# Spreading w1, w2 conversions and a, b units over steps 10 to 20, and reordering the loads and banks of M

## The chip, the cores and the metric

The kernel runs on one core of a Trainium2 chip. The metric is the device time of one execution in microseconds (us), as the median of the executions that were timed. TensorE (PE, with its weight loads PEld), VectorE (DVE), ScalarE (ACT) and GpSimd (POOL) each take their instructions in the order in which the program lists them; SyncE (SP) issues all DMAs of this kernel, also in order.

## The reference

Attention with a learned decay bias, then two feed-forward stages. All matrices arrive as 64-bit or 32-bit floats; the kernel splits each 32-bit operand into a rounded high word and a remaining low word (suffixes h and l) and adds three products (hh, hl, lh) for each product of matrices.

```python
bias   = -(cum[:, :, :, None] - cum[:, :, None, :])            # cum = cumsum(relu(s))
attn   = softmax(causal(q @ k.T * scale + min(bias, 0)))       # 4 batches x 8 heads, 576 x 576
x      = (attn @ v) heads side by side                         # 2304 x 512
h      = ((x @ w1) * (x @ w2)) @ w3                            # 1024 wide
y      = h @ w_out                                             # 512 wide
h2     = y @ w_in;  solu = h2 * softmax(h2);  ln = layer norm of solu, times g_ln
out    = ln @ w_out2                                           # 2304 x 512
```

The kernel multiplies w3 and w_out together first: M = w3 @ w_out, so that y = ((x @ w1) * (x @ w2)) @ M.

## The kernel before

**Order of the work.** The kernel is written in program order and a scheduler lays out each engine's list of instructions at build time: it prefers what stands earlier in the program, but takes a later instruction where, by its own reckoning of time, the earlier one isn't ready. The list is fixed then; on the chip an engine waits at the head of its list even where the next instruction could run. `tc.issue_after(ins)` (line 383 for one) forces an instruction behind another on the same engine.

**Steps.** Lines 534 to 598 run 36 steps. A step does the scores and softmax of one head (`qk_part`, `softmax_tile`, lines 180 to 214), the normalising and transposing of the head two before it (`normalise`, `tr_part`) and, for each pair of heads, probabilities times v (`av_parts`, line 265). Steps 0 to 9 take batch 0; from step 10 on, head h is done in step h + 2. Beside the heads run the a, b units of the batch before: `ab_unit(n, f, half)` at line 293 is 12 matmuls of x @ w1 for a block f of 128 columns and half the tokens, evicted by ACT to `a_sb` (line 315), and 12 of x @ w2, multiplied by `a_sb` on DVE into `g_sb` (line 323). `NF` (line 538) says how many units a step receives, and its 16 units of batch 0 (blocks f = 0 to 7, two halves) stand in steps 10 to 20.

**Conversions.** Blocks of w1 and w2 are loaded raw by `stage` (line 375, two buffers `stage` in this part) and converted from 64 bits by `to_f32` (ACT line 340, DVE lines 346, 347, 351) and split (`hi` on ACT line 93, `lo` on DVE line 98), which frees the buffer for the next load. `jobs` holds them in order: w1 block 0, w2 block 0, w1 block 1, and so on, 16 in all; unit block f needs jobs 2f+1 and 2f+2. `PUMP` (line 540) says how many conversions a step gets: steps 3, 5 and 6 one each, steps 10 to 15 two each, step 16 one. In steps, a conversion is also held behind the first softmax tile of that step's head (`behind`, line 195, line 399). The other half of the splitting, that of q and k, goes to POOL (`split_qk`, line 160).

**PSUM.** Steps use `bigtile` (tag A, two banks a tile: scores' first tile and `av`) and `smalltile` (tag B, one bank: everything else). Up to step 10 they are `psA` (2 tiles) and `psB` (4); from step 11 `psE` (1 tile, two banks) and `psF` (6).

**M.** After the steps the a, b units of the last batch run (lines 640 to 648) with the conversions of w_out and the first w3 blocks. Then psE and psF are closed and replaced by `psC` (tiles X, Y, Z, W for the second stage) and `psD` (4 small tiles), lines 651 to 655. Lines 896 to 906 build M: `load_g(0)` loads the first chunk of g, five `wf_load` load words of w_in that earlier steps had prepared, `load_g(1)` the second chunk; then for each of 8 blocks `m_unit(f)` does 24 matmuls of 512 columns and evicts MH and ML, `pump(AM[f])` converts two more w3 blocks (blocks 0 to 4) from four buffers, and `wf_words(f)` (line 885) splits one word for f below 6. After M, `x2_half` (line 698) multiplies g by M, and `h_pair` (line 846) the result by the words of w_in (`IT`, seven matrices in two halves, 14 words) on tiles X, Y, Z, W. The remaining eight of 22 words are those of w_out2 (OH, OL).

**End.** `out_unit(t)` (line 831) does 24 matmuls of 512 columns for 128 tokens, evicts them on ACT to `o` and stores them.

Of the kernel before, what the change touches and what calls it, by code (L numbers as in the profile page):

```python
# [26 lines left out]
def tile_attention_moe(  # L27
# [29 lines left out]
    for i in (2, 3, 1, 4, 0):  # L57
# [3 lines left out]

    dram = ctx.enter_context(tc.tile_pool(name="dram", bufs=1, space=DRAM))
    ps_ctx = ExitStack()
    PSP = [
        ps_ctx.enter_context(tc.tile_pool(name="psA", bufs=2, space=PSUM)),
        ps_ctx.enter_context(tc.tile_pool(name="psB", bufs=4, space=PSUM)),
    ]
    const = ctx.enter_context(tc.tile_pool(name="const", bufs=1, side="left"))
# [21 lines left out]

    def hi(dst, src, eng=None):
        if eng is None:
            nc.scalar.activation(out=dst, in_=src, func=AF.Copy)  # L93
        else:
            eng.tensor_copy(out=dst, in_=src)

    def lo(dst, src, hi_, eng=nc.vector):
        eng.tensor_tensor(out=dst, in0=src, in1=hi_.bitcast(F32), op=ALU.subtract)  # L98


    attn_ctx = ExitStack()
# [269 lines left out]
    loaded = []  # L371

    stg = [at, 2]

    def stage(src):
        raw = stg[0].tile([128, CW, 2], U32, tag="stage", bufs=stg[1], name="stage")
        dst = flat(raw)
        if len(src.shape) == 3:
            dst = dst.rearrange("p (c f) -> p c f", c=src.shape[1])
        if after[0] is None:  # L380
            nc.sync.dma_start(out=dst, in_=src)
        else:
# [155 lines left out]
    NF = {10: 3, 11: 0, 12: 3, 13: 0, 14: 3, 15: 2, 16: 2, 17: 0, 18: 1, 19: 1, 20: 1, 21: 2, 22: 2, 23: 2, 24: 2, 25: 2, 26: 2, 27: 2, 28: 2, 29: 2, 30: 2, 31: 2, 32: 2, 33: 2, 34: 3, 35: 3}  # L538
    PD, FS = 10, 0.5
    PUMP = {3: 1, 5: 1, 6: 1, 10: 2, 11: 2, 12: 2, 13: 2, 14: 2, 15: 2, 16: 1}  # L540
    PUMP.update((i, 1 if i < 30 else 2) for i in range(22, 34))
    fill = []
    late = []
    for st, (h, ph) in enumerate(steps):
# [3 lines left out]
        if st == 11:  # L548
            ps_ctx.close()
            PSP[:] = [  # L550
                ps_ctx.enter_context(tc.tile_pool(name="psE", bufs=1, space=PSUM)),
                ps_ctx.enter_context(tc.tile_pool(name="psF", bufs=6, space=PSUM)),
            ]

# [64 lines left out]
        w_job(w3L[f, :, 1024 * i:1024 * i + 1024], dst)  # L619

    def m_unit(f):
        ps = smalltile("m")
        for k in range(KF):
            H3, L3 = m_st[f, k // 4]
            for w_, o_ in ((H3, WOH), (H3, WOL), (L3, WOH)):
                nc.tensor.matmul(
                    ps, w_[:, k % 4], o_[:, k],
                    start=(k == 0 and w_ is H3 and o_ is WOH), stop=(k == KF - 1 and w_ is L3),
                )
        hi(MH[:, f], ps)  # L630
        lo(ML[:, f], ps, MH[:, f])
# [8 lines left out]
    for i in range(8):  # L640
# [8 lines left out]
    behind.clear()  # L649
    right0.close()  # L650
    ps_ctx.close()
    PSP[:] = [
        ctx.enter_context(tc.tile_pool(name="psC", bufs=1, space=PSUM)),
        ctx.enter_context(tc.tile_pool(name="psD", bufs=4, space=PSUM)),
    ]
    HD = DF // 2

    r2 = ctx.enter_context(tc.tile_pool(name="r2", bufs=1, side="right"))
# [171 lines left out]

    def out_unit(t):
        LH, LL = lt_t.pop(t)
        ps = smalltile("o")
        for k in range(KF):
            for l_, w_ in ((LH, OH), (LH, OL), (LL, OH)):
                nc.tensor.matmul(  # L836
                    ps, l_[:, k], w_[:, k],
                    start=(k == 0 and l_ is LH and w_ is OH), stop=(k == KF - 1 and l_ is LL),
                )
        o = p2.tile([128, DM], F32, tag="o", bufs=1, name="o")  # L840
        nc.scalar.activation(out=o, in_=ps, func=AF.Copy)
        nc.sync.dma_start(out=out[t * 128:t * 128 + 128], in_=o)

    NCH = NT // 2

    def h_pair(c):
# [5 lines left out]
        X, Y, Z, W = (PSP[0].tile([128, HD], F32, tag=n, name=f"h{n}") for n in "XYZW")  # L852
        h_mm(X, "A11", "B11", True)
        copy(h0[:, 0:HD], X)
        h_mm(Z, "S1", "T1", True)
# [24 lines left out]
    def wf_load(i):  # L880
        if i < len(WL):
            wf[i] = wpool.tile([128, CW], F32, tag="wf", bufs=5, name="wf")
            nc.sync.dma_start(out=wf[i], in_=wf_scr[WL[i]])
# [9 lines left out]
        lo(l_, t, h_, V)  # L893
        wf_load(i + 5)

    load_g(0)
    for i in range(5):
        wf_load(i)
    load_g(1)
    for f in range(nm[0], KF):  # L900
        m_unit(f)
        pump(AM[f])
        if f < 6:
            wf_words(f)
        if f == 5:
            split_g(0)
    mctx.close()
    p2 = ctx.enter_context(tc.tile_pool(name="p2", bufs=1, side="left"))
    OH = p2.tile([128, KF, DM], F32R, name="OH")
    OL = p2.tile([128, KF, DM], F32R, name="OL")  # L910
    x2_half(0, 0)
    x2_first(0)
    x2_half(0, 1)
    x2_second(0)
    split_g(1)
    for i in range(6, 14):
# [91 lines left out]
```

## Time and profile before

| | us |
|---|---|
| median of 3 executions (731.38 to 734.41) | 731.58 |
| the profiled execution, its own time | 732.8 |
| its span, first to last instruction | 731.1 |
| PE busy in the span | 714.2 (98%) |
| PEld busy | 631.5 (86%) |
| DVE busy | 507.7 (69%) |
| ACT busy | 470.4 (64%) |
| POOL busy | 95.2 (13%) |

The profile is of one execution. Times in rows are us from the span's start unless they are called ns. Matmuls overlap, so that neighbouring ones start before the one ahead has ended. A bracket at the end of a row of the timeline tells how long the engine had been idle and who released it.

### The profile page before, as it was taken

Reading aid. Unit: us, or ns where it says so; the run is one execution under the profiler, and the core shown is the slowest. Engines: PE = TensorE matmul, PEld = TensorE weight load, DVE = VectorE, ACT = ScalarE, POOL = GpSimd, SP = SyncE. Lnnn points to the kernel's source line nnn. Section 1 sums busy time; section 2 is a strip of 40 time slices with the busy share of each in tenths; the row PEclk is TensorE's granted clock in tenths of the full one; section 3 lists DMA queues with packets and bytes.
Section 4 is the critical chain, followed back from the end, with each engine's and each line's share of the span. In section 5 each row is a group of like instructions: output and inputs, shape, how many; then the busy total and the mean of one; then the engine's idle time right before and its main releaser. Section 6 shows DMA issues by size and latency. Waiting matters only on the chain.

```text
span 731.1 us, 12896 instructions
## 1 busy us (share of the span) xinstructions
PE 714.2 (98%) x4618; PEld 631.5 (86%) x4618; DVE 507.7 (69%) x1251; ACT 470.4 (64%) x977; POOL 95.2 (13%) x88
## 2 busy tenths in 40 slices
PE   9989998999999999999998999999999999999997
PEld 6669888889899999999997889988888988888886
DVE  7996989898777887822777966675747366563651
ACT  7996878798676777822544735576737465563742
POOL 3051322234121221000000000001000000000000
PEclk9999999999999999999999999999999999999999
DMA  5644555555476655514566933153324252302311
GB/s 124 190 135 132 156 164 146 164 148 127 140 205 184 207 164 175 179 62 161 185 204 201 378 114 101 59 116 87 79 66 102 45 133 68 87 19 68 66 36 43
DMA packets 79827, 95.50 MB, mean 131 GB/s; under 512 B 41418, under 2 KB 52682, under 8 KB 79764
## 3 DMA queue, kind: packets, MB, share of 16 engines
q1 hardware_dynamic: 79764, 94.69, 44.5%
q8 instruction: 36, 0.59, 0.3%
q14 instruction: 27, 0.22, 0.1%
HBM read 59.04 MB, written 20.14 MB: 108 GB/s over the span
## 4 chain that ended last, share of the span: by engine, by line
PE 81%; DVE 9%; DMA 5%; ACT 2%; issue 2%; SPq 0%; DVEq 0%; ACTq 0%
PE x L710 14%; PE o L836 14%; PE a L303 12%; PE b L303 11%; PE av L275 6%; PE hX L742 5%; PE tr L247 5%; DMA stage<-in_w_dram 4%; PE hZ L742 3%; PE sc L178 2%; PE sc L177 2%; PE hW L742 2%; PE hY L742 2%; DVE stage L351 2%; PE sc L169 1%
## 5 line engine op out<-in xcount | busy, mean ns | idle before, releaser
L190 ACT ACTIVATE P<-P,STAT 64x64 f32<-64x64 f32 (+4 forms) x160 | 88.5, 556 | 22.9 <-DVE STAT L186 22.3
L98 POOL TENSOR_TENSOR QK<-qk,QK 64x1152 fp32r<-64x1152 f32 x24 | 66.2, 2759 | 172.9 <-ACT QK L93 172.8
L710 PE MATMUL x<-gl,MH 128*128 128x256 f32 x288 | 80.4, 279 | 0.0
L710 PE MATMUL x<-gh,ML 128*128 128x256 f32 x288 | 80.2, 279 | 0.0
L710 PE MATMUL x<-gh,MH 128*128 128x256 f32 x288 | 79.9, 279 | 0.0
L303 PE MATMUL b<-xT0h,W 128*128 128x288 f32 x256 | 58.4, 301 | 3.5 <-DVE W L98 2.1
L303 PE MATMUL a<-xT0h,W 128*128 128x288 f32 x256 | 59.2, 306 | 0.0
L247 PE MATMUL tr<-ident,P 128*128 128x128 f32 x416 | 54.4, 275 | 3.5 <-DVE STAT L186 2.7
L303 PE MATMUL a<-xT1h,W 128*128 128x288 f32 x256 | 57.6, 300 | 0.0
L836 PE MATMUL o<-OH,lh 128*128 128x512 f32 x144 | 57.0, 396 | 0.2 <-DVE ll L98 0.2
L836 PE MATMUL o<-OH,ll 128*128 128x512 f32 x144 | 57.0, 396 | 0.0
L836 PE MATMUL o<-OL,lh 128*128 128x512 f32 x144 | 57.0, 396 | 0.0
L303 PE MATMUL b<-xT1h,W 128*128 128x288 f32 x256 | 56.4, 295 | 0.0
L710 PEld LDWEIGHTS x<-gl,MH 128*128 128x128 f32 x288 | 54.1, 188 | 1.5 <-DVE gl L98 0.2
L710 PEld LDWEIGHTS x<-gh,MH 128*128 128x128 f32 x288 | 53.9, 188 | 1.1
L710 PEld LDWEIGHTS x<-gh,ML 128*128 128x128 f32 x288 | 54.0, 188 | 0.9
L806 DVE COPY lt<-turned 128x2048 uint16<-128x2048 uint16 x16 | 22.0, 1373 | 45.4 <-DMA turned<-half 45.4
L247 PEld LDWEIGHTS tr<-ident,P 128*128 128x128 f32 x416 | 46.8, 141 | 5.4 <-issue 1.6
L323 DVE TENSOR_TENSOR g_sb<-b,a_sb 128x288 f32<-128x288 f32 x64 | 28.7, 450 | 31.6 <-PE b L303 21.5
L340 ACT ACTIVATE stage<-stage 128x512 f32<-128x512 f32 x56 | 37.1, 679 | 20.5 <-DMA stage<-in_w_dram 18.7
L226 ACT ACTIVATE P<-P,STAT 128x576 f32<-128x576 f32 x64 | 42.7, 717 | 10.5 <-DVE STAT L219 10.4
L315 ACT ACTIVATE a_sb<-a 128x288 f32<-128x288 f32 x64 | 25.7, 403 | 36.3 <-PE a L303 36.0
(191 smaller groups left out, 1984.1 us busy)
## 6 DMA issues: line engine op xcount, KB each, us to landing
stage<-in_w_dram SPq DMA_DIRECT2D x32, 512.0 KB
g_scr<-g_sb SPq DMA_DIRECT2D x32, 288.0 KB
stage<-in_wo_dram SPq DMA_DIRECT2D x16, 512.0 KB
qk<-in_qk_dram SPq DMA_DIRECT2D x24, 288.0 KB
QK<-QK SPq DMA_DIRECT2D x24, 288.0 KB
gl<-g_scr SPq DMA_DIRECT2D x24, 256.0 KB
wf<-wf_scr SPq DMA_DIRECT2D x22, 256.0 KB
out_dram<-o SPq DMA_DIRECT2D x18, 256.0 KB
```

What stands on the lines that cost most here:

```text
L98: eng.tensor_tensor(out=dst, in0=src, in1=hi_.bitcast(F32), op=ALU.subtract)
L190: ex = nc.scalar.activation(out=dst, in_=dst, func=AF.Exp, bias=st[0:rows, ti:ti + 1], scale=-1.0, accum_out=st[0:rows, 5 + ti:6 + ti],)
L226: nc.scalar.activation(out=dst, in_=src, func=AF.Copy, scale=r)
L247: last_tr[0] = nc.tensor.transpose(ps[:, 128 * n:128 * n + 128], pt[:, o:o + 128], ident)
L275: nc.tensor.matmul(st["ps"][64 * e:64 * e + 64, 448 + c0:448 + c1], vr[:, j, e], PT[(2 * p + e) % 4][:, o + c0:o + c1], **kw,)
L303: nc.tensor.matmul(ps, w_[:, c, fs], x_[:, c, sl], start=(c == 0 and w_ is WH and x_ is XH), stop=(c == KC - 1 and w_ is WL),)
L315: ab_last[0] = nc.scalar.activation(out=a_sb, in_=ps, func=AF.Copy).ins
L323: ab_last[1] = nc.vector.tensor_tensor(out=g[:, sl], in0=ps, in1=st["a"], op=ALU.mult).ins
L340: nc.scalar.activation(out=high.bitcast(F32), in_=high.bitcast(F32), func=AF.Copy, scale=2.0 ** -112)
L710: last = nc.tensor.matmul(ps[:, a], w_[:, k, m * 128:m * 128 + 128], g_[:, k % 2], start=(k == 0 and w_ is MH and g_ is GH), stop=(k == KF ...
L742: last_h[0] = nc.tensor.matmul(ps, x_[:, k], w_[:, k], start=first and k == 0 and x_ is XH and w_ is WH, stop=k == 1 and x_ is XL, skip_gr ...
L836: nc.tensor.matmul(ps, l_[:, k], w_[:, k], start=(k == 0 and l_ is LH and w_ is OH), stop=(k == KF - 1 and l_ is LL),)
```

## The change

The table of units goes from 3, 0, 3, 0, 3, 2, 2, 0, 1, 1, 1 to 2, 1, 2, 1, 2, 1, 2, 1, 2, 1, 1 for steps 10 to 20, that of conversions from 2, 2, 2, 2, 2, 2, 1 in steps 10 to 16 to 2, 1, 2, 1, 2, 1, 2, 1, 1 in steps 10 to 18. The double bank psE goes to the other side of PSUM and stays open over M; M's first block is computed in it, and it becomes tiles X and Y afterwards, while Z, W and psD replace psF. In M the loads of g and of words come behind the raw block that was staged last before them; only words 0 and 1 are split in M, words 2 to 13 behind the last w3 conversion, and the last four words of w_out2 behind the splits of the second stage's first chunk. The last `out_unit` works in two halves of 256 columns, each evicted and stored by itself.

```diff
@@ pools
-        ps_ctx.enter_context(tc.tile_pool(name="psA", bufs=2, space=PSUM)),
+        ps_ctx.enter_context(tc.tile_pool(name="psA", bufs=2, space=PSUM, side="right")),
@@ helpers: hi and lo note their instruction in last_hi[0], last_lo[0]; stage notes its DMA in last_stage[0]
+    def held(*ins):
+        order = ExitStack()
+        for i in ins:
+            order.enter_context(tc.issue_after(i))
+        return order
@@ steps
-    NF = {10: 3, 11: 0, 12: 3, 13: 0, 14: 3, 15: 2, 16: 2, 17: 0, 18: 1, 19: 1, 20: 1, 21: 2, ...}
+    NF = {10: 2, 11: 1, 12: 2, 13: 1, 14: 2, 15: 1, 16: 2, 17: 1, 18: 2, 19: 1, 20: 1, 21: 2, ...}
-    PUMP = {3: 1, 5: 1, 6: 1, 10: 2, 11: 2, 12: 2, 13: 2, 14: 2, 15: 2, 16: 1}
+    PUMP = {3: 1, 5: 1, 6: 1, 10: 2, 11: 1, 12: 2, 13: 1, 14: 2, 15: 1, 16: 2, 17: 1, 18: 1}
@@ step 11
-                ps_ctx.enter_context(tc.tile_pool(name="psE", bufs=1, space=PSUM)),
+                big_ctx.enter_context(tc.tile_pool(name="psE", bufs=1, space=PSUM, side="right")),
@@ m_unit
-        ps = smalltile("m")
+        ps = smalltile("m") if f else bigtile("m")[:, 0]
@@ second stage's banks
-    PSP[:] = [
-        ctx.enter_context(tc.tile_pool(name="psC", bufs=1, space=PSUM)),
-        ctx.enter_context(tc.tile_pool(name="psD", bufs=4, space=PSUM)),
-    ]
+    psp = {}
+    psp["Z"] = psp["W"] = ctx.enter_context(tc.tile_pool(name="psC", bufs=1, space=PSUM))
+    PSP[1] = ctx.enter_context(tc.tile_pool(name="psD", bufs=4, space=PSUM))
@@ M
-    load_g(0)
-    for i in range(5):
-        wf_load(i)
-    load_g(1)
     for f in range(nm[0], KF):
         m_unit(f)
-        pump(AM[f])
-        if f < 6:
-            wf_words(f)
+        if AM[f]:
+            pump(AM[f])
+            w3_last = last_hi[0], last_lo[0]
+        with held(last_stage[0]):
+            if f == 0:
+                load_g(0)
+            elif f == 1:
+                for i in range(5):
+                    wf_load(i)
+            elif f == 4:
+                load_g(1)
+        if 2 <= f < 4:
+            wf_words(f - 2)
         if f == 5:
             split_g(0)
     ...
+    big_ctx.close()
+    psp["X"] = psp["Y"] = ctx.enter_context(tc.tile_pool(name="psG", bufs=1, space=PSUM, side="right"))
     x2_half(0, 0)
     x2_first(0)
     x2_half(0, 1)
     x2_second(0)
+    words_last = last_hi[0], last_lo[0]
     split_g(1)
-    for i in range(6, 14):
-        wf_words(i)
+    with held(*w3_last):
+        for i in range(2, 14):
+            wf_words(i)
     load_g(2)
     ...
-            for i in range(14, 22):
+            for i in range(14, 18):
                 wf_words(i)
+            with held(*words_last):
+                for i in range(18, 22):
+                    wf_words(i)
@@ out_unit
+        for c0, c1 in ((0, DM),) if t < NT - 1 else ((0, DM // 2), (DM // 2, DM)):
+            ps = smalltile("o")[:, 0:c1 - c0]
             ... the matmuls on w_[:, k, c0:c1], the second part behind the first
+            nc.scalar.activation(out=o[:, c0:c1], in_=ps, func=AF.Copy)
+            nc.sync.dma_start(out=out[t * 128:t * 128 + 128, c0:c1], in_=o[:, c0:c1])
```

## Rows read from the trace of the kernel before

**Rows 1.** The page: busy time of each engine, its share of the span, instructions.

```profile
PE 714.2 (98%) x4618; PEld 631.5 (86%) x4618; DVE 507.7 (69%) x1251; ACT 470.4 (64%) x977; POOL 95.2 (13%) x88
```

**Rows 2.** Windows by stage: length, PE, PEld, DVE, ACT, POOL busy, clock, DMA, GB/s.

```profile
57.00:155.00 98.00, 92.66 (x665) 84.84 (x665) 84.34 (x237) 77.72 (x185) 26.29 (x9) 0.97 0.54 158
155.00:389.00 234.00, 234.00 (x1782) 217.97 (x1781) 166.46 (x438) 148.04 (x355) 34.60 (x13) 1.00 0.53 164
389.00:440.00 51.00, 48.15 (x228) 40.01 (x227) 39.47 (x70) 27.51 (x48) 0.00 (x0) 1.00 0.65 227
440.00:700.00 260.00, 260.00 (x1540) 229.43 (x1539) 158.35 (x321) 155.52 (x236) 17.12 (x25) 1.00 0.32 79
```

**Rows 3.** Timeline of PE, the three longest idle spans in 57 to 155.

```profile
92.67 0.52 PE L247 MATMUL tr<-ident,P 128*128 128x128 f32 x3 [1.40 <-DVE STAT L186]
...
120.53 0.40 PE L303 MATMUL b<-xT0h,W 128*128 128x288 f32 x1 [0.76 <-ACT W L93]
...
123.70 0.54 PE L303 MATMUL b<-xT0h,W 128*128 128x288 f32 x2 [2.09 <-DVE W L98]
```

**Rows 4.** Windows around the two stretches of lower clock (columns as in rows 2).

```profile
92.00:99.00 7.00, 6.21 (x34) 6.00 (x35) 6.92 (x25) 5.82 (x18) 3.93 (x1) 0.76 0.52 159
123.00:130.00 7.00, 6.30 (x36) 6.30 (x37) 5.15 (x22) 6.26 (x14) 1.24 (x1) 0.76 0.61 193
```

**Rows 5.** Waits of DVE in 57 to 155: us in total, times, longest.

```profile
DVE stage L346 <- DMA stage<-in_w_dram: 7.0, 5, 1.9
```

**Rows 6.** Timeline of DVE: the raw block ahead of a softmax, and head 12's tile.

```profile
91.42 0.43 DVE L346 TENSOR_SCALAR stage<-stage 128x512 uint32<-128x512 uint32 x1 [0.59 <-DMA stage<-in_w_dram]
91.76 0.62 DVE L186 CUSTOM_DVE_ANT_0 P<-sc,wmask 128x448 f32<-128x448 f32 x1
...
110.25 0.75 DVE L186 CUSTOM_DVE_ANT_0 P<-sc,lmask 128x576 f32<-128x576 f32 x1
```

**Rows 7.** Timeline of DVE and POOL, 118 to 124: head 13's tile and conversion 12.

```profile
118.06 0.75 DVE L186 CUSTOM_DVE_ANT_0 P<-sc,lmask 128x576 f32<-128x576 f32 x1
...
120.74 2.31 DVE L351 SCALAR_TENSOR_TENSOR stage<-stage 128x512 uint32<-128x512 uint32 x1
122.97 0.68 DVE L98 TENSOR_TENSOR W<-stage,W 128x512 fp32r<-128x512 f32 x1
...
119.86 2.64 POOL L98 TENSOR_TENSOR QK<-qk,QK 64x1152 fp32r<-64x1152 f32 x1 [5.71 <-ACT QK L93]
```

**Rows 8.** Conversion steps by shape, 57 to 155 (DVE), and one a unit's matmuls.

```profile
L347 DVE SCALAR_TENSOR_TENSOR stage<-stage 128x512 uint32<-128x512 uint32 x13 | 8.8, 682 | 0.0
...
99.42 1.60 PE a L303 x12
```

**Rows 9.** Timeline of PE and DVE around M's first matmul, and PE's wait at M's end.

```profile
391.99 0.50 PE L626 MATMUL m<-WOH,w3h 128*128 128x512 f32 x1 [2.24 <-DVE g_sb L323]
...
391.49 0.45 DVE L323 TENSOR_TENSOR g_sb<-b,a_sb 128x288 f32<-128x288 f32 x1
...
428.71 0.50 PE L626 MATMUL m<-WOH,w3h 128*128 128x512 f32 x1 [0.61 <-ACT w3h L93]
```

**Rows 10.** Timeline of DVE, 431 to 440, and PE's first use of T1's words.

```profile
434.75 0.69 DVE L98 TENSOR_TENSOR ML<-m,MH 128x512 fp32r<-128x512 f32 x1 [2.95 <-ACT MH L93]
439.86 0.69 DVE L98 TENSOR_TENSOR ML<-m,MH 128x512 fp32r<-128x512 f32 x1 [4.43 <-ACT MH L93]
...
456.36 0.40 PE L742 MATMUL hZ<-IT1h,XWh 128*128 128x512 f32 x1
```

**Rows 11.** DMAs of 395 to 425 in sum.

```profile
DMA packets 5453, 9.93 MB, mean 331 GB/s; under 512 B 488, under 2 KB 2536, under 8 KB 5451
```

**Rows 12.** The last eviction on ACT, and an eviction of 288 columns.

```profile
727.40 0.60 ACT L841 ACTIVATE o<-o 128x512 f32<-128x512 f32 x1 [5.00 <-PE o L836]
...
L315 ACT ACTIVATE a_sb<-a 128x288 f32<-128x288 f32 x14 | 5.5, 399 | 2.4 <-PE a L303 2.4
```

More of the change, by code (lines that the diff above doesn't have):

```diff
@@ L63, in tile_attention_moe @@
     ps_ctx = ExitStack()
+    big_ctx = ExitStack()
     PSP = [
-        ps_ctx.enter_context(tc.tile_pool(name="psA", bufs=2, space=PSUM)),
+        ps_ctx.enter_context(tc.tile_pool(name="psA", bufs=2, space=PSUM, side="right")),
         ps_ctx.enter_context(tc.tile_pool(name="psB", bufs=4, space=PSUM)),
@@ L92, in hi @@
         if eng is None:
-            nc.scalar.activation(out=dst, in_=src, func=AF.Copy)
+            last_hi[0] = nc.scalar.activation(out=dst, in_=src, func=AF.Copy).ins
         else:
@@ L97, in lo @@
     def lo(dst, src, hi_, eng=nc.vector):
-        eng.tensor_tensor(out=dst, in0=src, in1=hi_.bitcast(F32), op=ALU.subtract)
+        last_lo[0] = eng.tensor_tensor(out=dst, in0=src, in1=hi_.bitcast(F32), op=ALU.subtract).ins
+    last_hi, last_lo = [None], [None]
+    def held(*ins):
[3 more added lines that the diff above has]
+        return order
     attn_ctx = ExitStack()
@@ L373, in tile_attention_moe @@
     stg = [at, 2]
+    last_stage = [None]
     def stage(src):
@@ L380, in stage @@
         if after[0] is None:
-            nc.sync.dma_start(out=dst, in_=src)
+            last_stage[0] = nc.sync.dma_start(out=dst, in_=src).ins
         else:
             with tc.issue_after(after[0].ins):
-                nc.sync.dma_start(out=dst, in_=src)
+                last_stage[0] = nc.sync.dma_start(out=dst, in_=src).ins
         return raw
@@ L537, in tile_attention_moe @@
     steps += [(h if h < NH else None, h - 2 if h >= H + 2 else None) for h in range(H, NH + 2)]
-    NF = {10: 3, 11: 0, 12: 3, 13: 0, 14: 3, 15: 2, 16: 2, 17: 0, 18: 1, 19: 1, 20: 1, 21: 2, 22: 2, 23: 2, 24: 2, 25: 2, 26: 2, 27: 2, 28: 2, 29: 2, 30: 2, 31: 2, 32: 2, 33: 2, 34: 3, 35: 3}
+    NF = {10: 2, 11: 1, 12: 2, 13: 1, 14: 2, 15: 1, 16: 2, 17: 1, 18: 2, 19: 1, 20: 1, 21: 2, 22: 2, 23: 2, 24: 2, 25: 2, 26: 2, 27: 2, 28: 2, 29: 2, 30: 2, 31: 2, 32: 2, 33: 2, 34: 3, 35: 3}
     PD, FS = 10, 0.5
-    PUMP = {3: 1, 5: 1, 6: 1, 10: 2, 11: 2, 12: 2, 13: 2, 14: 2, 15: 2, 16: 1}
+    PUMP = {3: 1, 5: 1, 6: 1, 10: 2, 11: 1, 12: 2, 13: 1, 14: 2, 15: 1, 16: 2, 17: 1, 18: 1}
     PUMP.update((i, 1 if i < 30 else 2) for i in range(22, 34))
@@ L832, in out_unit @@
         LH, LL = lt_t.pop(t)
[L833 to L839, printed above, removed]
-        o = p2.tile([128, DM], F32, tag="o", bufs=1, name="o")
-        nc.scalar.activation(out=o, in_=ps, func=AF.Copy)
-        nc.sync.dma_start(out=out[t * 128:t * 128 + 128], in_=o)
+        o = p2.tile([128, DM], F32, tag="o", bufs=1, name="o")
+        last = None
+        for c0, c1 in ((0, DM),) if t < NT - 1 else ((0, DM // 2), (DM // 2, DM)):
+            ps = smalltile("o")[:, 0:c1 - c0]
+            with ExitStack() as order:
+                if last is not None:
+                    order.enter_context(tc.issue_after(last.ins))
+                for k in range(KF):
+                    for l_, w_ in ((LH, OH), (LH, OL), (LL, OH)):
+                        last = nc.tensor.matmul(
+                            ps, l_[:, k], w_[:, k, c0:c1],
+                            start=(k == 0 and l_ is LH and w_ is OH), stop=(k == KF - 1 and l_ is LL),
+                        )
+            nc.scalar.activation(out=o[:, c0:c1], in_=ps, func=AF.Copy)
+            nc.sync.dma_start(out=out[t * 128:t * 128 + 128, c0:c1], in_=o[:, c0:c1])
     NCH = NT // 2
@@ L851, in h_pair @@
         h0, h1 = ln_t[t0][0], ln_t[t1][0]
-        X, Y, Z, W = (PSP[0].tile([128, HD], F32, tag=n, name=f"h{n}") for n in "XYZW")
+        X, Y, Z, W = (psp[n].tile([128, HD], F32, tag=n, name=f"h{n}") for n in "XYZW")
         h_mm(X, "A11", "B11", True)
```

## The prediction

> **What bounds the kernel now.** Read the page's busy times first: PE works in 98% of the span, so nothing that only relieves another engine shortens it [rows 1]. What is left is 731.1 - 714.2 = 16.9 us without a matmul, and the stretches in which matmuls run at a lower clock. The second view, windows by stage, tells where these lie [rows 2]. From 57 to 155 us, where steps 10 to 20 run, PE is idle for 98.00 - 92.66 = 5.34 us and its clock averages 0.97. From 155 to 389, and again from 440 to 700, it is never idle. From 389 to 440, where M is made, it is idle for 2.85. The rest, some 9 us, is the first 57 us and what follows the last matmul, and of that the change touches only the last store. Third, the timeline of PE names what ended the idle spans: in steps 10 to 20 a transpose waited 1.40 us for a softmax tile on DVE, and the second half of one a, b unit waited 0.76 and then 2.09 for its converted weights [rows 3]. Behind both places the granted clock falls: over 7 us it averages 0.76, with PE at full clock before and after, so that part of each stretch ran at 1.2 GHz instead of 2.4 [rows 4]. The work lost is (1 - 0.76) x 7 = 1.7 us each. What there is to win in the stage is thus 5.34 + 3.4 = 8.7 us.
>
> **Steps 10 to 20.** Nothing is removed: 16 units and 13 conversions stand in the stage as before, each conversion with its load on SP's queue, three DVE steps and a split of 0.68 or less each and two ACT steps [rows 8]. What moves is when a conversion may start. I put the 1.40 us down to this: DVE's list has the softmax of 91.76 behind the first step of a conversion, that step waited 0.59 for its raw block, ran 0.43, and the softmax waited with it, and behind the softmax the transposes on PE [rows 3, 6]. It is one of five such waits of DVE for a raw block, 7.0 us together [rows 5]: with two buffers and two conversions per step, each block is loaded only when the conversion before it has freed its buffer. Alternating two and one gives each load a third more time, so I count this span and the lower clock behind it as gone: 1.40 + 1.7 = 3.1 us. The bound on the one side is nothing, since five such waits can come elsewhere; on the other all 8.7.
>
> The second place I leave as it is. It is conversion 12, the w2 block of f = 5, twelfth of the splits on DVE. Its split at 122.97 stood behind a step of conversion 13 that took 2.31 us instead of 0.68 while POOL split a head's q and k from 119.86 to 122.50 [rows 7, 8]: 1.62 us of the 2.09 are this collision. POOL's splits come one per head before and after the change, and which DVE step one meets isn't set by either table, so I take the value 0 between a gain of 0.76 + 2.09 + 1.7 = 4.5 us and a loss (rivals). The Trainium skill has a rule that speaks here against the change (SBUF — State Buffer, section "SBUF: two separate sides"): VectorE and GpSimd share one pair of SBUF ports as an exclusive lock, held for a whole instruction by whoever starts first. The trace agrees, in that the long step ends 0.55 us behind POOL's. By that rule, spreading the conversions over two more steps exposes them to more of POOL's splits, not fewer, and the stage could give nothing; that is the first rival.
>
> The units' new table puts one or two units (24 matmuls, 1.60 us for 12 [rows 8], so 3.2 us each) later: by the end of steps 10, 12, 14, 15, 16 and 17 it has handed out 1, 1, 1, 2, 2 and 1 fewer. PE's sum is the same.
>
> **M.** Before, M's first matmul waits 2.24 us for the last `g_sb`, a DVE step of 391.49 behind conversions in its list [rows 9]. The wait is for a bank: what the matmul reads was converted earlier, and the small tiles of psD lie where psF's were. The kept double bank had its last reader in the last step, before the 16 units of the last batch (16 x 3.2 = 51 us), so the first block can start behind the last unit: 2.24 us gone. The second block still needs a psD bank, 24 matmuls later, when that `g_sb` is long done. The 0.61 at 428.71 is a wait for a w3 block's high words [rows 9]. Blocks are now needed 2.24 sooner, but 12 of the words' splits leave DVE's and ACT's lists in M and raw blocks no longer queue on SP behind g and word loads. At 0.60 from start to start that is 7.2 us of DVE, in a stretch where DVE works 39.47 of 51 us [rows 2]; 7.2 exceeds 2.24 + 0.61 = 2.85, so I count 0.61 as gone as well. Bounds: nothing, if the supply of blocks eats what the bank gave, and 2.85.
>
> The words are paid elsewhere. After the last w3 split DVE is idle for 2.95 and 4.43, together 7.4 us, which hides 12 splits of 0.60, and PE first reads T1's words at 456.36 [rows 10]. Their loads, and those of eight words more, are 12 x 0.262 MB = 3.1 MB in the first instance, 9.5 us at 331 GB/s [rows 11]. From about 424 (431.10 less 7.2) they end at 434, and `load_g(0)`, 2.1 MB or 6.3 us, has some five of M's eight blocks as cover (48.15 us of PE for them and a little of the next stage [rows 2]). If that cover were gone, h_pair would wait for up to 9.5 us of loads, but T1 is read some 30 us after 424. I take nothing. The last four OH, OL words move behind the first chunk's splits; they are read first in the next round of the loop over chunks, behind all of `h_pair(0)` and `h_pair(1)`. I take nothing there either.
>
> **The end.** The last eviction takes 0.60 us; one of 288 columns takes 0.40 [rows 12], so half of it saves about 0.2. The last store moves half as much, 0.13 MB less, which is between nothing and 0.4 us at 331 GB/s [rows 11]; I take 0.2. The two halves do as many columns as before. Sum: 0.4 us.
>
> **Sum.** 3.1 + 2.85 + 0.4 = 6.35 us, say 6.4. The profiled execution took 732.8, of which 1.7 lie outside its span, and is 1.2 above the median of 731.58. 732.8 - 6.4 = 726.4 for such an execution; against the median, 725.2.
>
> **Rivals.** First, the stage gives nothing: raw blocks and POOL's collisions find other softmax tiles and other units to delay. For it speaks that DVE works 84.34 of 98 us there and ACT 77.72 [rows 2], little less than PE, so a slip has little room; against it, that from 155 to 389, with POOL's 13 splits and one conversion per step, the same slips never reach PE. Only M and the end stay: 731.6 - 3.25 = 728.3.
>
> Second, both places go, since a conversion that has its step to itself is not interleaved with the next one's steps. For it: the 2.09 came from conversion 13's step ahead of 12's split [rows 7]. That is 8.7 + 2.85 + 0.6 = 12.2, or 719.4.
>
> Third, slower: the conversions come too late. Conversion 12 is released in step 15 instead of 14, behind head 13's first tile (118.06) instead of head 12's (110.25), 7.8 us later [rows 6, 7], and before head 12's tile 9 conversions are released instead of 11, which allow 8 units instead of 10. If heads don't come sooner, PE runs out of units there and waits up to 7.8, plus 1.7 of lower clock: 9.5 - 3.25 = 6.2 us slower, 737.8. Against it: ahead of that tile PE has up to 2 x 3.2 us less to do and DVE two conversions of some 2.4 less, so the heads should come sooner by about as much. It decides from 7 of the 9.5 us on.
>
> Fourth, the scheduler lays M's lists so that the first block isn't at the bank's mercy yet stands behind another wait. Then only 0.4 to 3.5 is left of the forecast, which falls in the first rival's band.
>
> **How the numbers follow.** About 0.5%, 3.7 us, is what a measurement of this kernel can tell from no change: faster is below 727.9, slower above 735.2. The forecast, with one or the other place given back, has 0.44. Both places gone has 0.22; both count as faster, 0.66. Nothing from the stage, or M's gain lost, has 0.23 and falls within 0.5%. Too late conversions have 0.11. The range runs from 719.4, the second rival, to 731.0, which takes in the first rival with 2.7 us of M and the end lost again; it leaves out the third and the tail of the first.
>
> **What would show it.** In the trace after, M's first matmul within 0.3 us of the last a, b matmul, and no wait for a w3 block; PE busy for all of the window of M. In the stage, DVE's waits for raw blocks well below 7.0 us, and at most one stretch of lower clock. Wrong would be: idle spans of PE in the stage adding up to 5 us or more, ended by converted weights (third rival if behind a head's first tile, first if behind a raw block or POOL), or a wait of `h_pair` for its words.

## The result, and the profile after

The changed kernel takes 736.75 us (median of 9 executions, 735.94 to 737.74), the kernel before 732.57 beside it (9 executions, 731.38 to 735.77): a ratio of 1.0057, 95% interval 1.0042 to 1.0071. It is slower, by a little more than the 0.5% that a measurement can tell from no change. The profiled execution took 736.36, its span is 734.4.

The page's busy times of the kernel after (engine, us, share of the span, instructions):

```profile
PE 715.4 (97%) x4642; PEld 633.3 (86%) x4642; DVE 506.0 (69%) x1251; ACT 469.6 (64%) x978; POOL 93.9 (13%) x88
```

Its windows by stage (columns as in [rows 2]):

```profile
57.00:155.00 98.00, 87.18 (x613) 78.20 (x612) 82.11 (x221) 74.74 (x180) 25.02 (x9) 0.97 0.50 145
155.00:389.00 234.00, 234.00 (x1784) 217.93 (x1783) 163.47 (x447) 148.03 (x355) 34.66 (x13) 1.00 0.53 164
389.00:440.00 51.00, 51.00 (x250) 43.55 (x250) 43.67 (x77) 29.52 (x52) 0.00 (x0) 1.00 0.72 242
440.00:700.00 260.00, 260.00 (x1552) 229.86 (x1551) 155.34 (x318) 154.36 (x235) 17.01 (x25) 1.00 0.33 81
```

Set beside [rows 2], two stages moved, in opposite directions. In 57 to 155 PE is idle for 98.00 - 87.18 = 10.82 us, where it was 5.34. In 389 to 440 it is never idle, where it was 2.85. Milestones of the two traces put the sum together: the last a, b matmul ends at 396.68 instead of 389.75 (6.93 later); from there to the first matmul of `out_unit` it is 96.30 instead of 99.79 (3.49 gained); behind the last matmul the span lasts 3.25 instead of 3.81 (0.56 gained); 0.36 is lost between. 6.93 - 3.49 - 0.56 + 0.36 = 3.24, the growth of the span from 731.12 to 734.36.

The 6.93 is 5.48 of idle, 0.30 from a later start of the first a, b unit (59.33 against 59.03), and 1.15 of longer busy time on the same number of matmuls (326.53 against 325.38 between the first and the last a, b matmul), which no run takes apart. The lower clock costs the same as before: one stretch of some 8 us at a mean clock of 0.57, (1 - 0.57) x 8 = 3.4 us, where there were two of 1.7.

```profile
118.00:126.00 8.00, 7.25 (x31) 7.16 (x32) 6.62 (x24) 6.13 (x15) 0.38 (x2) 0.57 0.47 166
```

The timeline of PE after names what ended its three longest idle spans of the stage:

```profile
85.52 0.40 PE L312 MATMUL b<-xT0h,W 128*128 128x288 f32 x1 [1.75 <-DVE PT L96]
...
115.22 0.47 PE L186 MATMUL sc<-QK 128*128 128x512 f32 x1 [1.66 <-issue]
118.75 0.61 PE L312 MATMUL b<-xT0h,W 128*128 128x288 f32 x1 [2.70 <-ACT W L94]
```

The waits of [rows 3] are gone, and new ones stand in their place. The longest, 2.70, is the second half of a unit waiting for the high words of conversion 10 (the w2 block of f = 4). What ended the 1.66 the view doesn't tell. Where the 2.70 comes from stands in the timeline of DVE, with POOL's and ACT's rows of the same stretch below:

```profile
108.56 0.76 DVE L195 CUSTOM_DVE_ANT_0 P<-sc,lmask 128x576 f32<-128x576 f32 x1 [2.84 <-PE sc L187]
109.24 0.76 DVE L355 TENSOR_SCALAR stage<-stage 128x512 uint32<-128x512 uint32 x2
...
112.50 1.28 DVE L356 SCALAR_TENSOR_TENSOR stage<-stage 128x512 uint32<-128x512 uint32 x2
...
115.04 3.71 DVE L360 SCALAR_TENSOR_TENSOR stage<-stage 128x512 uint32<-128x512 uint32 x2
...
121.45 1.29 DVE L99 TENSOR_TENSOR W<-stage,W 128x512 fp32r<-128x512 f32 x2
...
115.32 2.88 POOL L99 TENSOR_TENSOR QK<-qk,QK 64x1152 fp32r<-64x1152 f32 x1 [2.77 <-ACT QK L94]
...
118.05 1.43 ACT L94 ACTIVATE W<-stage 128x512 fp32r<-128x512 f32 x2
```

Two things are to be read here. First, DVE was idle for 2.84 us and then took head 12's first tile, 108.56; only behind it do two first steps of conversions stand, as one row "x2". These are conversions 10 and 11, both given to step 14 by the new table and held behind that tile by `behind`. In the kernel before, conversion 10 belonged to step 13, was released behind head 11's tile (84.81) and was done by 105.77; now its last split ends at 122.13. Second, the two run in pairs, so that 10 waits for each step of 11, and their third step lies beside POOL's split of 115.32: 3.71 us for the pair, where two alone take 2 x 0.68 [rows 8].

In M the timeline of PE and DVE, and the last eviction:

```profile
396.38 0.29 PE L312 MATMUL b<-xT1h,W 128*128 128x288 f32 x1
396.51 0.39 PE L636 MATMUL m<-WOH,w3h 128*128 128x512 f32 x1
...
429.10 0.69 DVE L99 TENSOR_TENSOR w3l<-stage,w3h 128x512 fp32r<-128x512 f32 x1 [0.73 <-ACT w3h L94]
429.70 1.29 DVE L99 TENSOR_TENSOR IT1l<-wf,IT1h 128x512 fp32r<-128x512 f32 x2
...
439.38 0.68 DVE L99 TENSOR_TENSOR IT3l<-wf,IT3h 128x512 fp32r<-128x512 f32 x1
...
731.14 0.38 ACT L855 ACTIVATE o<-o 128x256 f32<-128x256 f32 x1 [2.40 <-PE o L851]
```

M's first matmul follows the last a, b matmul at once, against [rows 9]; the last w3 split is done at 429.8, and the words' splits fill what was DVE's idle time of [rows 10]. The last eviction takes 0.38 instead of 0.60 [rows 12].

### The profile page after: what moved, and what is told of

It reads as the page before. It is cut to its first block, busy times and chain, and to the rows that moved or that the text cites. A ratio compares the mean times of both kernels' runs of the same rounds, so it can differ in the third digit from the quotient of the medians.

```text
span 734.4 us, 12954 instructions
## 1 busy us (share of the span) xinstructions
PE 715.4 (97%) x4642; PEld 633.3 (86%) x4642; DVE 506.0 (69%) x1251; ACT 469.6 (64%) x978; POOL 93.9 (13%) x88
## 4 chain that ended last, share of the span: by engine, by line
PE 85%; DVE 9%; ACT 2%; DMA 1%; issue 1%; ACTq 0%; DVEq 0%
PE x L719 14%; PE o L851 14%; PE a L312 12%; PE b L312 12%; PE m L636 6%; PE av L284 5%; PE hX L751 5%; PE tr L256 5%; PE hZ L751 3%; PE sc L187 2%; PE sc L186 2%; DVE P L195 2%; PE hW L751 2%; PE hY L751 2%; DMA stage<-in_w_dram 1%
## 5 line engine op out<-in xcount | busy, mean ns | idle before, releaser
L199 ACT ACTIVATE P<-P,STAT 128x320 f32<-128x320 f32 (+4 forms) x160 | 88.4, 555 | 32.0 <-DVE STAT L195 31.3
L851 PE MATMUL o<-OH,lh 128*128 128x512 f32 (+1 forms) x152 | 58.4, 384 | 0.2 <-DVE ll L99 0.2
L851 PE MATMUL o<-OH,ll 128*128 128x512 f32 (+1 forms) x152 | 58.3, 383 | 0.0
L851 PE MATMUL o<-OL,lh 128*128 128x512 f32 (+1 forms) x152 | 58.3, 383 | 0.0
L284 PE MATMUL av<-PT,VT 128*64 128x64 f32 (+4 forms) x384 | 48.8, 394 | 0.0
L186 PE MATMUL sc<-QK 128*128 128x448 f32 (+3 forms) x144 | 43.1, 313 | 5.9 <-issue 1.7
```

What stands on the lines that cost most here:

```text
L186: nc.tensor.matmul(view, t[:, 0, q0:q0 + rows], t[:, 3, c0:c0 + w], start=True, stop=False)
L199: ex = nc.scalar.activation(out=dst, in_=dst, func=AF.Exp, bias=st[0:rows, ti:ti + 1], scale=-1.0, accum_out=st[0:rows, 5 + ti:6 + ti],)
L284: nc.tensor.matmul(st["ps"][64 * e:64 * e + 64, 448 + c0:448 + c1], vr[:, j, e], PT[(2 * p + e) % 4][:, o + c0:o + c1], **kw,)
L851: last = nc.tensor.matmul(ps, l_[:, k], w_[:, k, c0:c1], start=(k == 0 and l_ is LH and w_ is OH), stop=(k == KF - 1 and l_ is LL),)
```

## The experiments

**The theories.** T: conversion 10 is released too late, behind head 12's tile, and everything in the stage follows from that. R1: the stage lost by collisions of DVE's steps with POOL's splits of q and k, which the new order only moved onto a worse place. R2: the units' table lost it. R3: the reordering of M takes something back elsewhere. Below, "tables" means `NF` and `PUMP`. Ratios are to the kernel before on the same chip, with 95% intervals. "Stage" is the time from the first a, b matmul to the last one in the profiled execution: 330.72 before, 337.35 after.

**1. M and the end without the tables** (after, with both old tables).

```diff
-    NF = {10: 2, 11: 1, 12: 2, 13: 1, 14: 2, 15: 1, 16: 2, 17: 1, 18: 2, ...}
-    PUMP = {..., 10: 2, 11: 1, 12: 2, 13: 1, 14: 2, 15: 1, 16: 2, 17: 1, 18: 1}
+    NF = {10: 3, 11: 0, 12: 3, 13: 0, 14: 3, 15: 2, 16: 2, 17: 0, 18: 1, ...}
+    PUMP = {..., 10: 2, 11: 2, 12: 2, 13: 2, 14: 2, 15: 2, 16: 1}
```

> The changed kernel with both tables (units and conversions) put back as they were; M's order and banks and the halved last store stay. If the tables alone made it slower, PE's idle time between 57 and 160 us is back at some 5.3 us (10.8 with the new tables) and the time is 732.6 - 3.5 (M) - 0.4 (end) = 728.7. If the new sides of the banks or the new M already lay the steps out differently, the idle time is neither of the two and the time lies anywhere between 727 and 736.

Measured: 729.35 us, 0.9957 (0.9941 to 0.9973). M stands gapless behind the last unit, and the old wait of 2.09 is back in the stage. The window of 57 to 160, and a row of PE's waits there (us in total, times, longest):

```profile
57.00:160.00 103.00, 97.40 (x710) 88.97 (x709) 88.39 (x253) 83.08 (x202) 26.76 (x10) 0.98 0.52 155
```

```profile
PE b L312 <- DVE W L99: 2.1, 1, 2.1
```

R3 falls: M and the end alone gain 0.43%, about 3.1 us, close to the 3.25 of the sum.

**2. The tables without M and the end** (before, with both new tables; the diff of experiment 1 reversed).

> The kernel before with the two new tables and nothing else. Theory (tables cost the stage some 6.6 us, M and the end give back 3.9 independently): 732.6 + 6.6 = 739, with M's waits of 2.24 and 0.6 us still there. Rival (the parts depend on each other, M gains only since its stage starts later): below 737.

Measured: 739.61 us, 1.0097 (1.0077 to 1.0117), stage 336.65. The same two views:

```profile
57.00:160.00 103.00, 91.98 (x655) 82.70 (x654) 86.17 (x239) 78.47 (x190) 24.98 (x9) 0.97 0.51 153
```

```profile
PE b L303 <- ACT W L93: 2.7, 1, 2.7
```

The wait for conversion 10 is there without anything of M. 0.97 - 0.43 = 0.54% against 0.57% for both: the two parts add.

**3. Only the units' table** (after, with the old `PUMP`).

> The changed kernel with the old table of conversions and the new one of units. Theory (conversions 10 and 11 are released behind head 12's first tile instead of head 11's, and PE runs out of units until they are done): the wait for converted weights around 116 us goes, PE idles 3 to 6 us in 57 to 160, and the time is 727 to 730. Rival (units handed out later leave PE without filler): still some 10 us idle and 736. Rival (any new order draws new slips): anything between.

Measured: 733.01 us, 1.0003 (0.9983 to 1.0023), stage 331.70. The waits for conversions are gone, and one of 3.57 us is new, behind a copy of transposes on DVE that stood behind a conversion's split beside POOL:

```profile
PE a L312 <- DVE PT L96: 3.6, 1, 3.6
```

The time lies above the 727 to 730 that theory T gave. So R2 is not all of it, but not nothing: against experiment 1 the units cost 0.46%.

**4. Only the conversions' table** (after, with the old `NF`).

> The changed kernel with the old table of units and the new one of conversions. Theory (late release of conversions): the wait stays, PE idles 9 to 12 us in 57 to 160, 735 to 738. Rival (units): 5 to 6 us idle and 728 to 730.

Measured: 734.20 us, 1.0027 (1.0013 to 1.0041), stage 334.86, and the longest stretch of lower clock that any run has in the stage, 10.24 us from 111.5. PE waits 1.58 for conversion 10, whose split ends at 117.55. Against experiment 1 this is 0.70%: by the medians the larger part of the loss is the conversions', but the intervals of experiments 3 and 4 overlap.

**5. One conversion moved back** (after, with conversion 10 again in step 13; 16 conversions, and 9 steps that receive them, as in the change).

```diff
-    PUMP = {..., 12: 2, 13: 1, 14: 2, 15: 1, 16: 2, 17: 1, 18: 1}
+    PUMP = {..., 12: 2, 13: 2, 14: 1, 15: 1, 16: 2, 17: 1, 18: 1}
```

> The changed kernel with one conversion moved in its table: step 13 gets two and step 14 one, so that conversion 10 is released behind head 11's first tile (86 us) and no longer behind head 12's (109 us). Late release as the cause of the 2.70 us wait and of the 6.8 us of lower clock behind it: both go or shrink, PE idles 5 to 8 us in 57 to 160 instead of 10.8, 730 to 733. Layout (any order draws its own slips): no tie to this wait, 733 to 739.

Measured: 729.14 us, 0.9957 (0.9942 to 0.9972), stage 329.57. The window, and DVE's timeline with head 11's tile, conversion 10's last split and head 12's tile:

```profile
57.00:160.00 103.00, 98.27 (x719) 88.81 (x718) 91.83 (x249) 83.70 (x202) 27.53 (x10) 1.00 0.54 159
```

```profile
86.17 0.74 DVE L195 CUSTOM_DVE_ANT_0 P<-sc,lmask 128x576 f32<-128x576 f32 x1
...
103.12 0.69 DVE L99 TENSOR_TENSOR W<-stage,W 128x512 fp32r<-128x512 f32 x1 [0.91 <-ACT W L94]
...
108.94 0.76 DVE L195 CUSTOM_DVE_ANT_0 P<-sc,lmask 128x576 f32<-128x576 f32 x1 [0.47 <-PE sc L187]
```

Up to 96 us PE's waits are those of after. Then conversion 10 is done at 103.81 instead of 122.13, PE doesn't wait between 113 and 119, and the clock never falls. The one moved conversion is worth 1.0057 - 0.9957 = 1.0%, 7.3 us; POOL's splits are all still there.

**6. The hold alone** (after; conversions 10 and 11 stay in step 14, but aren't held behind head 12's tile).

```diff
+            kept = list(behind)
+            if st == 14:
+                behind.clear()
             pump(PUMP.get(st, 0))
+            behind[:] = kept
```

> The changed kernel with its own tables, where only the conversions of step 14 (10 and 11) are no longer held behind that step's first softmax tile. Late release: as before, 730 to 733. If not the hold but the loads (two buffers, freed by conversion 9) or the scheduler's own order kept them back, they still end near 122 us and the time stays within 736 to 738.

Measured: 729.89 us, 0.9965 (0.9952 to 0.9978), stage 330.23. Conversion 10 ends at 103.24 and 11 at 109.15, and PE's idle time in 57 to 160 is 103.00 - 97.14 = 5.86:

```profile
57.00:160.00 103.00, 97.14 (x712) 88.07 (x712) 92.88 (x248) 82.95 (x201) 27.71 (x10) 1.00 0.53 157
```

What T says of the release is shown: two conversions in step 14 do no harm by themselves; that their release hangs on a tile that comes late does. Whether that alone makes the loss is another question (experiment 15).

**7. Two of POOL's splits gone** (after, with the low words of q, k of heads 14 and 15 on DVE, the one of 115.32 among them).

```diff
-        lo(t[64:128, 1::2], raw, t[64:128, 0::2], G)
+        lo(t[64:128, 1::2], raw, t[64:128, 0::2], V if h in (14, 15) else G)
```

> The changed kernel with the low words of q and k of heads 14 and 15 made on DVE instead of POOL, which takes away POOL's two instructions at 110 and 115 us and adds some 2.5 us to DVE. Collision as the cause: the step of 3.11 us at 115.6 is 0.7 again, conversion 10 ends 2 us sooner, 734 to 735. Late release: PE has nothing to do in any case until the conversion has gone through, 736 to 738.

Measured: 733.32 us, 1.0012 (0.9999 to 1.0025), stage 334.07. Conversion 10 still ends at 120.79 and PE still waits there:

```profile
PE sc L186 <- ACT PT L94: 2.3, 1, 2.3
PE b L312 <- ACT W L94: 1.7, 1, 1.7
```

These two splits are worth 0.45%, less than half of what experiments 5 and 6 gave, but more than T allowed: it gave 736 to 738. So R1 holds in part. The seven other splits in the stage are still on POOL here; experiment 15 takes them away too.

**8. Conversions earlier still** (after, with the old `NF` and conversions in steps 8 and 9 too).

```diff
-    PUMP = {3: 1, 5: 1, 6: 1, 10: 2, 11: 1, 12: 2, 13: 1, 14: 2, 15: 1, 16: 2, 17: 1, 18: 1}
+    PUMP = {3: 1, 5: 1, 6: 1, 8: 1, 9: 1, 10: 2, 11: 2, 12: 2, 13: 2, 14: 2, 15: 1}
```

> The changed kernel with the old table of units and conversions released sooner than in either: one each in steps 8 and 9, two each in steps 10 to 14, one in 15. Late release: PE never waits for converted weights, the waits of 0.75 and 2.09 near 120 us go too, 57 to 160 idles 2 to 4 us, 725 to 728, faster than with the old tables (729.4). If DVE's and ACT's load is what binds there, the heads of steps 10 to 13 are held up instead and the time is 729 to 733.

Measured: 729.00 us, 0.9961 (0.9944 to 0.9978), no better than experiment 1. The windows of the stage and of a stretch ahead of its first unit:

```profile
57.00:160.00 103.00, 100.52 (x736) 90.83 (x735) 87.94 (x251) 82.76 (x205) 27.54 (x10) 0.98 0.52 155
50.00:62.00 12.00, 10.36 (x51) 7.60 (x51) 8.32 (x21) 7.28 (x18) 3.69 (x2) 0.57 0.43 138
```

PE waits for no conversion any more, the 2.09 of [rows 3] included, and idles only 2.48 in 57 to 160. The price stands ahead of that: in steps 8 and 9, between the batches, the two conversions delay softmax and transposes, the clock falls to 0.57 over 12 us, and the first unit starts at 65.61 instead of 60.05. The last a, b matmul ends at 389.99, in experiment 1 at 389.80.

**9 and 10. The halves of M.** One kernel is before with only the kept bank for M's first block; the other is experiment 1 with that block in a small tile, so that the order of loads and words alone is left.

```diff
-        ps = smalltile("m")
+        ps = smalltile("m") if f else bigtile("m")[:, 0]
```

> The kernel before with M's first block in the kept double bank (which then becomes X and Y) and nothing else of the change. If the wait of 2.24 us ahead of M was for a bank, M's first matmul follows the last a, b matmul without a gap; but blocks are then needed sooner with the same supply, and the wait at M's end grows from 0.6 to about 2 us: 732.4 - 1 = 731 to 732. If the supply had room, 729.5 to 730.

> The changed kernel with the old tables, and M's first block in a small tile as before: only the order of M's loads and words, the banks' sides and the halved store are left. If order and bank each pay their own wait: the gap ahead of M is back at 2.2 us, none at M's end, 729.4 + 2.3 = 731.7. If the order alone pays nothing: 732 to 733.

Measured: 733.27 us, 0.9998 (0.9976 to 1.0019), and 733.24 us, 0.9995 (0.9975 to 1.0015). The totals settle nothing; each gain is smaller than its interval. The traces do: the first two rows are the bank alone, with M at once behind the last unit and the wait for a w3 block still there, and the last is the order alone, with the wait ahead of M.

```profile
394.90 0.39 PE L627 MATMUL m<-WOH,w3h 128*128 128x512 f32 x1
...
431.56 0.50 PE L627 MATMUL m<-WOH,w3h 128*128 128x512 f32 x1 [0.46 <-ACT w3h L94]
```

```profile
393.58 0.50 PE L636 MATMUL m<-WOH,w3h 128*128 128x512 f32 x1 [1.52 <-DVE g_sb L332]
```

From the last a, b matmul to the first of `out_unit` the bank alone takes 98.43 us, the order alone 98.15, both 96.30, neither 99.79.

**11 to 15. No splits of q and k on POOL in the steps.** The low words of q, k go to DVE for every head, in five kernels: experiment 5, before, experiment 1, experiment 3 and after.

```diff
-        lo(t[64:128, 1::2], raw, t[64:128, 0::2], G)
+        lo(t[64:128, 1::2], raw, t[64:128, 0::2], V)
```

> The kernel that releases conversion 10 in step 13 (729.1), with the low words of q and k of all heads on DVE instead of POOL. If the collisions cost DVE about what the work itself costs (10.8 us of stretched steps in nine heads against nine steps of some 1.2), DVE's load stays the same and the waits of PE at 84 us (1.24) and 93.6 us (0.92) shrink: 726 to 728.5. If DVE's list is what binds, 729 to 733.

> The kernel before, with the low words of q and k of all heads on DVE instead of POOL. The wait of 2.09 us near 121 us was put down to a step stretched from 0.7 to 2.31 by POOL: then it falls below 0.8 and the time to 729 to 731. If the late release of conversion 12 causes it, the wait stays above 1.5 and the time at 731.5 to 734.

> M's new order and banks, the halved store and the old tables, with the low words of q and k on DVE instead of POOL. Beside the kernel with conversion 10 in step 13 and no POOL splits (0.989 of the kernel before): if spreading is worth something once collisions and the late release are gone, this one stays at 0.994 to 0.998; if taking the splits off POOL is all there is, it reaches 0.988 to 0.991 too.

> The new table of units with the old one of conversions, with the low words of q and k on DVE instead of POOL. With POOL it was 1.000, 0.4% above the old tables, with a wait of 3.57 us at 83 us behind a step that POOL stretched to 3.0. If that collision is the price of the units' table, the wait goes and the ratio is 0.988 to 0.993; if units handed out later are, it stays at 0.996 to 1.002.

> The changed kernel as it is, with the low words of q and k on DVE instead of POOL. Late release as the cause of its loss: the wait for conversion 10 behind head 12's tile stays, 1 us shorter at most, ratio 0.999 to 1.003. If the collisions were the cause: 0.988 to 0.993, like the version with conversion 10 in step 13.

Measured (all rows but the first have M and the end as in after; the stages are of the profiled executions):

| tables | splits on POOL | stage | splits on DVE | stage |
|---|---|---|---|---|
| before, M as before | 1 | 330.72 | 735.61, 1.0033 (1.0009 to 1.0056) | 329.31 |
| old | 0.9957 | 329.75 | 729.83, 0.9967 (0.9954 to 0.9981) | 328.94 |
| new units, old conversions | 1.0003 | 331.70 | 728.78, 0.9965 (0.9948 to 0.9983) | 326.40 |
| new, as in after | 1.0057 | 337.35 | 729.63, 0.9971 (0.9954 to 0.9988) | 328.42 |
| new, conversion 10 in step 13 | 0.9957 | 329.57 | 725.42, 0.9887 (0.9860 to 0.9915) | 323.90 |

The last is the fastest kernel of all, 1.1% faster than before. Five readings. First, with old tables the splits on DVE bring nothing (in before's form they cost 0.33%), and the wait for conversion 12 stays, in before's form and in experiment 1's:

```profile
126.76 0.40 PE L303 MATMUL b<-xT0h,W 128*128 128x288 f32 x1 [2.66 <-ACT W L93]
```

```profile
122.88 0.40 PE L312 MATMUL b<-xT0h,W 128*128 128x288 f32 x1 [2.54 <-ACT W L94]
```

Second, after keeps its wait for conversion 10 without any POOL instruction in the stage, and yet is 0.86% faster than with them (its window, then PE's timeline):

```profile
57.00:160.00 103.00, 97.85 (x711) 88.73 (x708) 90.76 (x256) 83.10 (x201) 0.00 (x0) 0.98 0.53 157
```

```profile
115.43 0.47 PE L186 MATMUL sc<-QK 128*128 128x512 f32 x1 [1.48 <-ACT PT L94]
...
118.87 0.40 PE L312 MATMUL b<-xT0h,W 128*128 128x288 f32 x1 [2.61 <-ACT W L94]
```

The window of the fastest kernel, whose PE has only 2.07 us of idle time there:

```profile
57.00:160.00 103.00, 100.93 (x748) 91.15 (x748) 95.08 (x270) 87.56 (x215) 0.00 (x0) 1.00 0.58 163
```

Third, what POOL cost DVE is read from the groups by shape in 57 to 160 (busy time, mean ns of one), after with POOL's nine splits and after without:

```profile
L356 DVE SCALAR_TENSOR_TENSOR stage<-stage 128x512 uint32<-128x512 uint32 x13 | 12.1, 943 | 0.3 <-ACT stage L349 0.3
L360 DVE SCALAR_TENSOR_TENSOR stage<-stage 128x512 uint32<-128x512 uint32 x13 | 11.1, 868 | 0.0
L355 DVE TENSOR_SCALAR stage<-stage 128x512 uint32<-128x512 uint32 x13 | 9.8, 767 | 4.2 <-DMA stage<-in_w_dram 4.2
...
L227 DVE TENSOR_SCALAR STAT<-STAT 128x5 f32<-128x5 f32 x9 | 3.6, 395 | 3.6 <-ACT P L199 3.6
```

```profile
L99 DVE TENSOR_TENSOR QK<-qk,QK 64x1152 fp32r<-64x1152 f32 x10 | 13.6, 1356 | 1.1 <-ACT QK L94 0.9
L360 DVE SCALAR_TENSOR_TENSOR stage<-stage 128x512 uint32<-128x512 uint32 x13 | 8.9, 694 | 0.1
L356 DVE SCALAR_TENSOR_TENSOR stage<-stage 128x512 uint32<-128x512 uint32 x13 | 8.7, 683 | 0.0
...
L355 DVE TENSOR_SCALAR stage<-stage 128x512 uint32<-128x512 uint32 x13 | 5.4, 425 | 2.5 <-DMA stage<-in_w_dram 2.4
...
L227 DVE TENSOR_SCALAR STAT<-STAT 128x5 f32<-128x5 f32 x10 | 1.6, 165 | 0.6 <-ACT P L199 0.5
```

The three conversion steps take 33.0 us beside POOL and 23.0 without it, and one small step of the normalising (L227) 3.6 instead of 1.6: together 12.0 us more. Nine splits of q and k at 1.36 would take DVE 12.2. What POOL took off DVE it thus gave back in longer steps.

Fourth, the two causes are not one: late release costs 7.8 us of stage with POOL's splits (337.35 - 329.57) and 4.5 without (328.42 - 323.90); POOL's splits cost 8.9 with the late release (337.35 - 328.42), 5.7 without it (329.57 - 323.90) and 0.8 with old tables (329.75 - 328.94); by the medians 0.86%, 0.70% and less than nothing (0.9957 against 0.9967). Neither is the first cause. Against the old tables in the same column the new ones lose 1.00% with both causes present and nothing measurable with either one gone (0.9957 against 0.9957, 0.9971 against 0.9967). Stages are compared here rather than medians since in four of the five kernels (all but the fastest) the profiled execution has a stretch of lower clock at 51 to 54 us, ahead of the stage, where the tables differ in nothing; their first unit starts at 61.6 to 63.8 us, in the fastest kernel at 60.67. What of the medians' 6.1 us between the last two rows is that start isn't settled.

Fifth, not all of what was expected came. After without POOL's splits has 0.9971, between the 0.999 to 1.003 of late release and the 0.988 to 0.993 of collisions: neither alone explains the loss. The new units with the old conversions have 0.9965, in the band of "units handed out later", though the wait of 3.57 us behind the stretched split is gone; that the collisions are their price rests on the stage, which is 2.5 us shorter than with old tables (328.94 - 326.40), where it was 1.95 longer with POOL's splits (331.70 - 329.75). And before without POOL's splits kept its wait, as late release has it, but at 735.61 us is slower than either theory gave; its first unit starts at 63.81, 4.8 us later than in before. Experiments 4, 5, 6 and 10 came out up to 1 us faster than expected, 9 and 11 some 1 us slower.

## Why the prediction was wrong

It gave 725.2 us and 0.11 to the case that came, its third rival, slower by late conversions. The miss lies in the stage alone: the prediction had it 3.1 us shorter, and it became 6.6 us longer; M and the end, forecast at 3.25, gave 3.69. The sign that it had named came too: PE's idle spans of the stage add up to 10.82 us, over the 5 that were to be the limit. Point by point:

**M: right, a little undersized.** Predicted -2.85; the stretch from the last unit to `out_unit` shrank by 3.49. Both waits of [rows 9] are gone. "Nothing" for the words' later splits and loads held: T1's words fill DVE's idle time, and PE never waits for them. The halves gave 1.36 and 1.64 by themselves, together 3.00 of 3.49, so that each needs the other for the rest.

**The end: right.** Predicted -0.4, measured -0.56 behind the last matmul.

**The first place of steps 10 to 20: the mechanism was there, but wasn't what counts.** DVE's waits for raw blocks did fall, from the 7.0 of [rows 5] to 4.2. The view puts another 2.6, for one `g_sb`, down to a load, but the last matmul of that unit ended at 102.71 and the `g_sb` began at 102.80, so that it waited for PE as long:

```profile
DVE stage L355 <- DMA stage<-in_w_dram: 4.2, 5, 1.2
DVE g_sb L332 <- DMA stage<-in_w_dram: 2.6, 1, 2.6
```

The 1.40 of [rows 3] and the lower clock behind it are gone as counted. But "1.40 + 1.7 = 3.1 us" was the whole balance of the stage in the sum, and as such it failed: idle spans of 1.75, 1.66 and 2.70 came, the lower clock cost 3.4 us at the last of them, and the stage lost 6.6 us (337.35 - 330.72).

**The second place: wrong reading.** "1.62 us of the 2.09 are this collision" took the long step ahead of the split for the cause. With no split on POOL the same wait is 2.66 and 2.54 (experiments 12 and 13), though there DVE has the split of q and k, 1.36 us, in its own list; with conversions released earlier it is gone, with POOL's splits in place (experiment 8). Conversion 12, too, was late because it was released behind head 12's tile, 110.25 in [rows 6]: the kernel before had a small case of what the change made large. Read that way, [rows 3] would have spoken for the third rival.

**The third rival: right place, wrong weight.** The prediction counted it: "before head 12's tile 9 conversions are released instead of 11, which allow 8 units instead of 10". It then set against it that "PE has up to 2 x 3.2 us less to do and DVE two conversions of some 2.4 less, so the heads should come sooner by about as much". This is the first step that failed. Head 12's tile came at 108.56 instead of 110.25, 1.7 us sooner and not 6.4. It comes 20 to 26 us behind head 11's in all seventeen kernels, while heads 9 to 11, 13 and 14 follow the one before them within 2 to 12. So what is released behind it is late in every layout, and the free choice is how much goes ahead of it. Why it stands there I can only argue: its scores need the one double bank, which probabilities times v of the pair before take (99.6 to 103.3 in after, read out by DVE until 105.27); the scores then start at 107.75, behind a, b matmuls in PE's list. No run took that wait away.

The price was close: 9.5 us of rival against 7.3 us for the one conversion (experiment 5 against after). I named conversion 12 behind head 13's tile as the one that decides; it was 10 behind head 12's.

**The first rival** (collisions find other victims) came too, and weighs as much. The second step that failed is "which DVE step one meets isn't set by either table, so I take the value 0": POOL's splits cost 0.8 us of stage with the old tables and 8.9 with the new ones (the fourth reading above). With old conversions the new units cost 0.46% with POOL's splits and nothing without (1.0003 against 0.9957, 0.9965 against 0.9967). The Trainium skill (SBUF — State Buffer, "SBUF: two separate sides") has GpSimd and those VectorE instructions that have two SBUF inputs, or run in a 2-port mode, exclude each other from a shared pair of ports for a whole instruction. The runs agree as far as they go: the conversion steps take 425, 683 and 694 ns with no POOL instruction in the stage, and 767, 943 and 868 on average beside nine.

**What the change was good for** shows only with both causes taken away: with the splits on DVE and conversion 10 in step 13 the spread tables have a stage of 323.90 us, the old ones 328.94 with the splits on DVE too.

## What to carry to other kernels

Before spreading work over more steps, list for each piece what releases it, and find the event that comes late whatever one does; count how much is released ahead of that event, and keep that count when the table is changed. A long instruction beside a wait isn't its cause until the wait goes with it: look at when the late item was allowed to start. Where two causes are suspected, take each away alone and both together: here either one gone ended the loss against the old tables, and only both gone gave a gain. And a part given to a second engine is no help where it lengthens the first engine's instructions by as much.

## What the runs showed of the hardware

The lower clock of PE follows some idle spans and not others, also in the same code. In the kernel before, the 2.24 us ahead of M were followed by full clock, and the 1.40 at 92.67 by a mean of 0.76 over 7 us [rows 2 to 4, 9]. The twelve executions of experiment 3's kernel had mean clocks from 0.993 (736.35 us) to 1.000 (728.80 us). Experiments 11 and 15 have the same tables up to step 12 and the same list of PE for the first 100 us, and PE idles in the same short spans between 48 and 53 us (0.57, 0.66, 0.80 and 0.43 in the first, 0.57, 0.66 and 0.82 in the second). From 50 to 58 the granted clock was 1.00 in the one and 0.58 in the other, so that this one ran mostly at 1.2 GHz instead of 2.4 and lost (1 - 0.58) x 8 = 3.4 us of work. The windows of the first and of the second:

```profile
50.00:58.00 8.00, 6.36 (x44) 4.38 (x45) 4.87 (x14) 5.73 (x16) 0.00 (x0) 1.00 0.50 141
```

```profile
50.00:58.00 8.00, 6.92 (x25) 4.13 (x26) 4.30 (x12) 4.90 (x14) 0.00 (x0) 0.58 0.45 140
```

A single profile of such a kernel can thus be some 3 us off by where the clock happened to fall.

A split of q and k (64 x 1152) takes 1.36 us on DVE and, in the stage of after, 2.65 to 3.07 on POOL. A conversion step of DVE that meets it there ends shortly behind it: 2.31 us instead of 0.68 in [rows 7], 0.55 behind POOL's end.
